# Dense work beside attention in steps of 512 tokens in place of 256, with weight conversions spread, the product with v in one run, and tau loaded first

## The chip, the cores and the metric

One core of one Trainium2 chip runs the kernel; the other cores are idle. The metric is the device time of one execution in microseconds. TensorE (PE, with its weight loads PEld), VectorE (DVE), ScalarE (ACT), GpSimd (POOL) and SyncE (SP) each run their own queue of instructions in order and wait for one another by semaphores. All DMAs of this kernel are issued from SP.

## The reference

Sparse attention followed by two dense blocks, all in float32. Four batches, eight heads, 576 tokens, head size 64:

```python
scores = q @ k.T / 8
thresh = max(scores) - tau
scores = where(scores >= thresh, scores, -1e9)
attn = exp(scores - max(scores)); attn = attn / (sum(attn) + 1e-9)
x = (attn @ v), heads joined: 2304 tokens x 512
h = x @ w_in1                      # 512 -> 2048
g = h where h >= 1, 0 where h <= -1, else (h + 1)**2 / 4
x = g @ w_out1                     # 2048 -> 512
h = x @ w_in2
out = (h * clip(h + 3, 0, 6) / 6) @ w_out2
```

The weights arrive as 64-bit floats, of which the kernel reads the two 32-bit halves.

## The kernel before, in words

**Attention** goes by jobs: 16 of them, one for each batch and pair of heads (`jobs`), with five row blocks each (128, 128, 128, 128 and 64 query rows), so 80 steps, and three more steps to drain. In a step `t` the generator `attention` (L407) issues, with a `yield` after each part: the scores of a block (`em_scores`: matmuls at L284, a pass out of PSUM with the row minimum of the negated scores at L296, exp at L300, a small add at L303, mask and row sum at L306); the turned tail of the block two steps back (`em_tail`); up to three chunks of the product with v (`pv_run(3)`, L420); at certain blocks the normalisation of the job before (`em_norm`, which writes x to DRAM and marks the job done) or the turning of the next q or k; then the transposes of the block one step back, for two heads (`em_pt`), with two more product chunks between them (`pv_run(2)`, L438). A job's blocks are gathered in two groups, and each group's product with v has five chunks (`pv_chunk`, L361), for 32 groups in all.

**Dense work beside attention** is `dense1` (L605). It does part of the first dense block, the first 10 of its 16 blocks of hidden units (`NF1`), for the 512 main tokens of batches 0 to 2, in six groups of 256 tokens (`GRP`). A float32 product is made from three passes (`hi*hi`, `hi*lo`, `lo*hi`) in the type fp32r. `em_h` makes a hidden block: 4 x 3 matmuls of 128x128 weights by 256 tokens (L485) into one PSUM bank, Q2 while attention runs (`H_TAGS`), then two ScalarE steps and one VectorE step of the activation (L494 to L496) and its split in `gh` and `gl` (L502, L503). `em_part` does the second matmul (L542): two of the four output blocks side by side in bank Q3, summed over ten hidden blocks, then copied out (L551, L553) and written to `x2p`. `split_x` loads x (L460) and splits it (L468, L469). `steps` lists which output pieces follow which hidden block; what is left after the last hidden block is issued by `behind` in the next phase. The sum over the other six hidden blocks is added there.

**The order** around this is set by hand. The main loop (L711) runs attention from yield to yield. Until batch 0 is ready it converts weights: `weights.half()` once a step and twice in every third step. Each conversion of one weight block has two halves: `split_a` (ScalarE L111 and L114, GpSimd L115, VectorE L122) and `split_b` (VectorE L128, GpSimd L130, L133 and L137; beside dense work ScalarE L135 in place of L133). Loads run up to three blocks ahead (`RAW`). From then on each yield earns 0.57 of credit, which pays for pieces of dense work at 0.33 each (three matmuls of 256 columns); weights not yet converted are converted when `ahead1` asks for them. Tile's planner orders each engine's queue with a timeline of its own from this program, so issue order is a priority and not the exact order; `after` pins one instruction behind another on its engine. `pin_mlp` pins the first matmul of a dense piece behind an attention matmul.

**Afterwards** the same first dense block follows for batch 3 and the 256 tail tokens, then the remaining six hidden blocks for batches 0 to 2, then the second dense block, all in steps of 512 tokens (256 for the tail group).

Of the kernel before, what the change touches and what calls it, by code (L numbers as in the profile page):

```python
# [18 lines left out]
def kernel(  # L19
# [12 lines left out]
    nc = tc.nc  # L32
# [23 lines left out]
    mt = mt_es.enter_context(tc.tile_pool(name="mt", bufs=2, side="right"))  # L56
# [8 lines left out]
    xd, x2p, x2d = ([dram.tile([128, KD, n], F32, name=f"{nm}{w}") for w, n in enumerate(WIDE)]  # L65
                    for nm in ("xd", "x2p", "x2d"))

    def narrow(t, g):
        return t[g // 2][:, :, (g % 2) * GRP:(g % 2 + 1) * GRP]
# [34 lines left out]
    def split_a(kind, m, f):  # L104
# [12 lines left out]
        else:  # L117
# [4 lines left out]
        V.tensor_scalar(out=c, in0=c, scalar1=3, scalar2=0x3FFFFFFF,  # L122
                        op0=ALU.logical_shift_left, op1=ALU.bitwise_and)
        wc[kind, m, f] = (hi, lo, c, t, r)

    def split_b(kind, m, f):
        hi, lo, c, t, r = wc.pop((kind, m, f))
        V.scalar_tensor_tensor(out=c, in0=t[:, :, 1], scalar=0xC0000000, in1=c,  # L128
                               op0=ALU.bitwise_and, op1=ALU.bitwise_or)
# [141 lines left out]
    def em_scores(j, i):  # L271
# [135 lines left out]
    def attention():  # L407
# [3 lines left out]
        for t in range(n + 3):  # L411
# [8 lines left out]
            pv_run(3)  # L420
# [17 lines left out]
            pv_run(2)  # L438
# [12 lines left out]
    def split_x(key, kks=range(KD)):  # L451
        m, g, ph = key
        r = xs.setdefault(key, [])
        for kk in kks:
            if kk < len(r):
                continue
            if ph == 1:
                if kk % 2 == 0:
                    t = mt.tile([128, 2, GRP], F32, tag="io", name="xst", bufs=2)
                    nc.sync.dma_start(out=t, in_=narrow(xd, g)[:, kk:kk + 2, :])  # L460
                pool, n, bufs, src = mt, GRP, 1, t[:, kk % 2]
            else:
                pool, n, bufs = wide["x"], WIDE[g], 2
                src = pool.tile([128, n], F32, tag="xst", name="xst", bufs=3)
                nc.sync.dma_start(out=src, in_=(x2d if m == 1 else xd)[g][:, kk, :])
# [10 lines left out]
    def em_h(key, m, f):  # L476
        cnt["h"] += 1
        n = GRP if key[2] == 1 else WIDE[key[1]]
# [3 lines left out]
        for kk in range(KD):  # L482
# [6 lines left out]
            if kk < KD - 1:  # L489
                yield 0.33  # L490
        hp_, hb = (mt, HOLD) if key[2] == 1 else (wide["g"], MLAG + 1)
        r = hp_.tile([128, n], F32, tag="r", name="r", bufs=2)
# [38 lines left out]
    def em_part(key, half, f):  # L531

        gh, gl = gs[key, f] if half == 0 else gs.pop((key, f))
        wh, wl = wsp["o", 0, f]
        if f == 0:
            acc[key] = bank("Q3")
        a = acc[key]
        for i in range(2):
            c = slice((2 * half + i) * 128, (2 * half + i + 1) * 128)
            o = a[:, i * GRP:(i + 1) * GRP]  # L540
            for x, (l, r) in enumerate(((wh[:, c], gh), (wh[:, c], gl), (wl[:, c], gh))):
                mm = T.matmul(o, l, r, start=(f == 0 and x == 0 and i == 0),  # L542
                              stop=(f == NF1 - 1 and x == 2 and i == 1), skip_group_check=True)
                if x == 0:
                    pin_mlp(mm)
            if i == 0:
                yield 0.33
        if f == NF1 - 1:
            ob = mt.tile([128, 512], F32, tag="io", name="ob", bufs=2)
            if half:  # L550
                S.activation(out=ob, in_=acc.pop(key), func=ACTF.Copy)  # L551
            else:
                V.tensor_copy(out=ob, in_=acc.pop(key))  # L553
            nc.sync.dma_start(
# [267 lines left out]
```

## Time and profile before

| | us |
|---|---|
| median of 3 runs | 1200.21 |
| lowest, highest | 1199.99, 1202.96 |
| the profiled execution | 1200.08 |
| its span, first to last instruction | 1198.3 |

The page gives, for each engine, the time in which it was busy, as a share of the span. Groups of instructions are named by line, engine, operation and tiles (written <- read), with shapes in partitions x elements; then the count, the busy time, the mean duration, and how long the engine was idle just before them and what ended that. A matmul's duration in the profile includes its way through the array, where the next one already runs behind it, so the distance between the starts of two matmuls is what one costs in a run. The chain of waits is the work that ended last, followed back from the last instruction in a stretch.

### The profile page before, as it was taken

Reading aid. Unit: us, or ns where it says so; the run is one execution under the profiler, and the core shown is the slowest. Engines: PE = TensorE matmul, PEld = TensorE weight load, DVE = VectorE, ACT = ScalarE, POOL = GpSimd, SP = SyncE. Lnnn points to the kernel's source line nnn. Section 1 sums busy time; section 2 is a strip of 40 time slices with the busy share of each in tenths; the row PEclk is TensorE's granted clock in tenths of the full one; section 3 lists DMA queues with packets and bytes.
Section 4 is the critical chain, followed back from the end, with each engine's and each line's share of the span. In section 5 each row is a group of like instructions: output and inputs, shape, how many; then the busy total and the mean of one; then the engine's idle time right before and its main releaser. Section 6 shows DMA issues by size and latency. Waiting matters only on the chain.

```text
span 1198.3 us, 17942 instructions
## 1 busy us (share of the span) xinstructions
PE 1138.7 (95%) x6656; PEld 906.7 (76%) x6656; DVE 579.6 (48%) x1196; ACT 627.5 (52%) x1217; POOL 418.8 (35%) x397
## 2 busy tenths in 40 slices
PE   4877799998999999999999999999999999999998
PEld 3444477876777787777888988888888888888886
DVE  3899865456555565553652575555740121121111
ACT  4667766565665665664665676654542222233222
POOL 1767531110111111112673666656742213222221
PEclk9999889999999999999999999999999999999999
DMA  4444421212111222003431244453210010010000
GB/s 114 117 133 135 128 81 30 51 50 59 54 35 31 59 59 68 21 20 107 149 103 47 81 136 150 152 168 98 88 43 15 1 58 9 1 44 2 18 1 35
DMA packets 106791, 82.43 MB, mean 69 GB/s; under 512 B 66512, under 2 KB 90576, under 8 KB 106704
## 3 DMA queue, kind: packets, MB, share of 16 engines
q1 hardware_dynamic: 106704, 81.29, 23.0%
q8 instruction: 52, 0.85, 0.3%
q14 instruction: 35, 0.29, 0.1%
HBM read 63.96 MB, written 17.30 MB: 68 GB/s over the span
## 4 chain that ended last, share of the span: by engine, by line
PE 83%; DVE 6%; ACT 4%; DMA 3%; SPq 2%; issue 2%; POOL 0%; ACTq 0%; DVEq 0%
PE Q L485 33%; PE P L527 26%; PE Q L542 7%; PE Q L361 6%; PE P L284 5%; PE Q L244 5%; DVE p L306 2%; DVE p L296 2%; DMA w_raw<-in_moe_w_in_dram 1%; PE P L244 1%; ACT e L300 1%; DMA w_raw<-in_moe_w_out_dram 1%; DVE w_c L122 1%; ACT r L494 1%; DVE w_c L128 1%
## 5 line engine op out<-in xcount | busy, mean ns | idle before, releaser
L503 POOL TENSOR_TENSOR gl<-r,gh 128x512 fp32r<-128x512 f32 (+1 forms) x190 | 205.9, 1084 | 641.7 <-ACT gh L502 624.1
L485 PE MATMUL Q<-xh,wih 128*128 128x512 f32 (+1 forms) x760 | 264.5, 349 | 0.7 <-ACT xh L468 0.5
L485 PE MATMUL Q<-xl,wih 128*128 128x512 f32 (+1 forms) x760 | 257.8, 339 | 0.2 <-DVE xl L469 0.2
L485 PE MATMUL Q<-xh,wil 128*128 128x512 f32 (+1 forms) x760 | 257.6, 339 | 0.0
L499 DVE SCALAR_TENSOR_TENSOR r<-r,Q 128x512 f32<-128x512 f32 (+1 forms) x80 | 50.7, 633 | 248.9 <-ACT r L498 248.8
L485 PEld LDWEIGHTS Q<-xh,wih 128*128 128x128 f32 x760 | 144.7, 191 | 29.9 <-issue 10.6
L502 ACT ACTIVATE gh<-r 128x512 fp32r<-128x512 f32 (+1 forms) x190 | 99.9, 526 | 121.5 <-PE P L527 53.3
L485 PEld LDWEIGHTS Q<-xl,wih 128*128 128x128 f32 x760 | 144.8, 191 | 16.5 <-DVE xl L469 0.7
L485 PEld LDWEIGHTS Q<-xh,wil 128*128 128x128 f32 x760 | 144.6, 190 | 15.6 <-issue 0.5
L296 DVE TENSOR_SCALAR_CACHE_REDUCE p<-P 128x576 f32<-128x576 f32 x144 | 104.1, 753 | 80.0 <-PE Q L244 71.5
L306 DVE SCALAR_TENSOR_TENSOR p<-p,th,e 128x576 f32<-128x576 f32 x144 | 130.9, 923 | 24.0 <-ACT e L300 17.4
L244 PE MATMUL Q<-ident,p 128*128 128x128 f32 (+1 forms) x656 | 113.8, 287 | 21.1 <-DVE p L306 10.1
L300 ACT ACTIVATE e<-p,nm 128x576 f32<-128x576 f32 x144 | 109.8, 773 | 32.7 <-DVE p L296 31.6
L498 ACT ACTIVATE r<-Q,three 128x512 f32<-128x512 f32 (+1 forms) x80 | 51.4, 643 | 143.4 <-PE Q L485 140.3
L244 PEld LDWEIGHTS Q<-ident,p 128*128 128x128 f32 (+1 forms) x656 | 74.6, 143 | 63.0 <-DVE p L306 11.7
L284 PE MATMUL P<-kt,qt 64*128 64x288 f32 (+1 forms) x640 | 109.1, 450 | 13.7 <-DVE p L296 7.5
L496 DVE SCALAR_TENSOR_TENSOR r<-r,Q 128x256 f32<-128x256 f32 (+1 forms) x110 | 55.0, 500 | 131.9 <-ACT r L495 129.5
L527 PE MATMUL P<-woh,gh 128*128 128x512 f32 x288 | 111.9, 390 | 0.6 <-DVE ob L580 0.6
L527 PE MATMUL P<-wol,gh 128*128 128x512 f32 x288 | 112.2, 390 | 0.0
L527 PE MATMUL P<-woh,gl 128*128 128x512 f32 x288 | 110.9, 390 | 0.0
L130 POOL TENSOR_TENSOR w_c<-w_c,w_raw 128x512 int32<-128x512 int32 x64 | 87.4, 1366 | 39.3 <-DVE w_c L128 28.1
L327 ACT ACTIVATE Gf<-Q 128x512 f32<-128x512 f32 x128 | 75.0, 591 | 48.6 <-PE Q L244 48.5
(81 smaller groups left out, 1865.2 us busy)
## 6 DMA issues: line engine op xcount, KB each, us to landing
w_raw<-in_moe_w_in_dram SPq DMA_DIRECT2D x32, 512.0 KB, 3.8
w_raw<-in_moe_w_out_dram SPq DMA_DIRECT2D x32, 512.0 KB, 3.6
xst<-xd SPq DMA_DIRECT2D x28, 256.0 KB, 3.2
kn<-in_k_dram SPq DMA_DIRECT2D x32, 128.0 KB, 2.6
qn<-in_q_dram SPq DMA_DIRECT2D x32, 128.0 KB, 2.6
vn<-in_v_dram SPq DMA_DIRECT2D x32, 128.0 KB, 2.6
xd<-xu SPq DMA_DIRECT2D x16, 256.0 KB, 2.5
x2d<-ob SPq DMA_DIRECT2D x16, 256.0 KB, 3.4
```

What stands on the lines that cost most here:

```text
L130: x = G.tensor_tensor(out=c.bitcast(I32), in0=c.bitcast(I32), in1=r, op=ALU.add)
L244: x = T.transpose(out, in_, ident)
L284: mm = T.matmul(o, qt[j][r, c], kt[j][r, k0:k0 + HS], start=True, stop=True, skip_group_check=True)
L296: V.tensor_scalar(out=p[:, x], in0=s[:, :, 0:HS], scalar1=-1.0, scalar2=3e38, op0=ALU.mult, op1=ALU.min, accum_out=nm[:, x:x + 1])
L300: S.activation(out=e, in_=p[:, x], func=ACTF.Exp, bias=nm[:, x:x + 1], scale=-1.0)
L306: V.scalar_tensor_tensor(out=p[:, x], in0=p[:, x], scalar=th[:, x:x + 1], in1=e, op0=ALU.is_le, op1=ALU.mult, accum_out=zt[j][:, z:z + 1])
L327: S.activation(out=f[:, h, :, d0:d0 + 128], in_=tm.rearrange("p (c n) -> p c n", c=4), func=ACTF.Copy)
L485: mm = T.matmul(h, l[:, kk * 128:(kk + 1) * 128], r, start=(x == 0), stop=(x == 3 * KD - 1))
L502: x = S.activation(out=gh, in_=r, func=ACTF.Copy)
L503: y = G.tensor_tensor(out=gl, in0=r, in1=f32(gh), op=ALU.subtract)
L527: T.matmul(a, l, r, start=(first and x == 0), stop=(last and x == 2))
L542: mm = T.matmul(o, l, r, start=(f == 0 and x == 0 and i == 0), stop=(f == NF1 - 1 and x == 2 and i == 1), skip_group_check=True)
```

## The change

The groups of dense work beside attention are 512 tokens, one for each of batches 0 to 2. `em_h` makes 4 x 3 matmuls of 512 columns. `em_part` makes one output block of 512 tokens for one hidden block; a bank holds one output block only, so its sum is split in two runs of five hidden blocks (`SUB`): the first is written to a new DRAM tensor `x2q`, and the second reads it back, adds it, and writes `x2p`. Output pieces alternate with the quarters of a hidden block, 18 behind (`OFF`), and while a batch isn't ready, waiting pieces are issued. A piece of three 512-column matmuls costs 0.62 of credit. Conversions go one half a step, before dense work begins and beside it, pinned behind the step's exp (ScalarE) and masking (VectorE). All five chunks of a product with v are issued at one place. Tau's load is the first DMA. Pools are cut to fit.

```diff
-    GRP = 256
-    NG = (NB - 1) * MAIN // GRP
+    NG = NB - 1
...
+    SUB = 5
...
-        V.tensor_scalar(out=c, in0=c, scalar1=3, scalar2=0x3FFFFFFF,
-                        op0=ALU.logical_shift_left, op1=ALU.bitwise_and)
+        x = V.tensor_scalar(out=c, in0=c, scalar1=3, scalar2=0x3FFFFFFF,
+                            op0=ALU.logical_shift_left, op1=ALU.bitwise_and)
+        if mode["att"]:
+            after(x, pins["V"])
...
-            S.activation(out=e, in_=p[:, x], func=ACTF.Exp, bias=nm[:, x:x + 1], scale=-1.0)
+            pins["S"] = S.activation(out=e, in_=p[:, x], func=ACTF.Exp, bias=nm[:, x:x + 1], scale=-1.0)
...
-            V.scalar_tensor_tensor(out=p[:, x], in0=p[:, x], scalar=th[:, x:x + 1], in1=e,
-                                   op0=ALU.is_le, op1=ALU.mult, accum_out=zt[j][:, z:z + 1])
+            pins["V"] = V.scalar_tensor_tensor(
+                out=p[:, x], in0=p[:, x], scalar=th[:, x:x + 1], in1=e,
+                op0=ALU.is_le, op1=ALU.mult, accum_out=zt[j][:, z:z + 1])
...
-            pv_run(3)
             yield
...
-            pv_run(2)
+            pv_run(5)
...
+            n = WIDE[g]
             if ph == 1:
-                if kk % 2 == 0:
-                    t = mt.tile([128, 2, GRP], F32, tag="io", name="xst", bufs=2)
-                    nc.sync.dma_start(out=t, in_=narrow(xd, g)[:, kk:kk + 2, :])
-                pool, n, bufs, src = mt, GRP, 1, t[:, kk % 2]
+                pool, bufs = xt, 1
+                src = mt.tile([128, n], F32, tag="io", name="xst", bufs=2)
...
+    def em_part(g, sub, i, f):
+
+        key = (0, g, 1)
+        lasti = i == KD - 1
+        gh, gl = gs.pop((key, f)) if lasti else gs[key, f]
         wh, wl = wsp["o", 0, f]
+        if f % SUB == 0:
+            cnt["a"] += 1
+            acc[key] = bank("Q3" if mode["att"] or cnt["a"] % 2 else "Q1")
+            if sub:
+                pbs[key] = mt.tile([128, MAIN], F32, tag="io", name="pb", bufs=2)
+                nc.sync.dma_start(out=pbs[key], in_=x2q[g][:, i, :])
         a = acc[key]
+        c = slice(i * 128, (i + 1) * 128)
+        for x, (l, r) in enumerate(((wh[:, c], gh), (wh[:, c], gl), (wl[:, c], gh))):
+            mm = T.matmul(a, l, r, start=(f % SUB == 0 and x == 0), stop=(f % SUB == SUB - 1 and x == 2))
+            if x == 0:
+                pin_mlp(mm)
+        if f % SUB == SUB - 1:
+            del acc[key]
+            if sub:
+                ob = pbs.pop(key)
+                V.tensor_tensor(out=ob, in0=a, in1=ob, op=ALU.add)
+            else:
+                ob = mt.tile([128, MAIN], F32, tag="io", name="ob", bufs=2)
+                if i % 2:
+                    S.activation(out=ob, in_=a, func=ACTF.Copy)
+                else:
+                    V.tensor_copy(out=ob, in_=a)
+            nc.sync.dma_start(out=(x2p if sub else x2q)[g][:, i, :], in_=ob)
...
+    outs = [(g, sub, i, sub * SUB + f) for g in range(NG) for sub in range(NF1 // SUB)
+            for i in range(KD) for f in range(SUB)]
+    n_out = len(outs)
+    OFF = 4 * SUB - 2
+    HOLD = max(u // 4 for u in [OFF + o - 4 * (g * NF1 + f) for o, (g, _, i, f) in enumerate(outs) if i == KD - 1])
+    PIECE = 0.62
...
                 while not ready(g):
-                    yield None
+                    if outs[0][0] < g:
+                        weights.upto(2 * NF1)
+                        em_part(*outs.pop(0))
+                        yield PIECE
+                    else:
+                        yield None
                 split_x(key)
             ahead(n, f)
+            h = em_h(key, 0, f)
+            for kk in range(KD):
+                next(h, None)
+                if f == NF1 - 1 and kk == KD - 1:
+                    xs.pop(key)
+                    if g + 1 < NG and ready(g + 1):
+                        split_x((0, g + 1, 1))
...
+                yield PIECE
+                if n_out - len(outs) < 4 * n + kk + 1 - OFF:
+                    em_part(*outs.pop(0))
+                    yield PIECE
...
+    nc.sync.dma_start(out=taus[:, 2:3], in_=tau.to_broadcast([128, 1]))
     load_k(0)
     load_q(0)
-    nc.sync.dma_start(out=taus[:, 2:3], in_=tau.to_broadcast([128, 1]))
...
                 weights.half()
-                if mode["t"] % 3 == 0:
-                    weights.half()
             if not ready(0):
                 continue
             mode["mlp"] = True
+        elif mode["step"] and weights.done < 2 * NF1:
+            mode["step"] = False
+            weights.half()
```

## Rows read from the trace of the kernel before

**Rows 1.** The page, part 1: busy us, share of the span, instructions

```profile
PE 1138.7 (95%) x6656; PEld 906.7 (76%) x6656; DVE 579.6 (48%) x1196; ACT 627.5 (52%) x1217; POOL 418.8 (35%) x397
```

**Rows 2.** Busy by stage (us): PE, PEld, DVE, ACT, POOL; granted clock; DMA

```profile
42.00:140.00 98.00, 75.52 (x466) 44.35 (x466) 87.68 (x190) 67.03 (x135) 65.93 (x65) 0.92 0.44 124
...
160.00:553.00 393.00, 384.18 (x2842) 295.55 (x2838) 211.05 (x583) 238.30 (x518) 55.16 (x79) 0.99 0.16 43
```

**Rows 3.** L303 (once a step of attention) by stage: us, DVE busy (count)

```profile
42.00:140.00 98.00, 5.58 (x17) 0.92 0.44 124
...
160.00:534.00 374.00, 11.87 (x53) 0.99 0.17 45
```

**Rows 4.** Groups, 42 to 140 us: count | busy, mean | idle before

```profile
L306 DVE SCALAR_TENSOR_TENSOR p<-p,th,e 128x576 f32<-128x576 f32 x31 | 36.6, 1197 | 6.2 <-ACT e L300 5.3
...
L122 DVE TENSOR_SCALAR w_c<-w_c 128x512 uint32<-128x512 uint32 x15 | 11.4, 763 | 1.2 <-POOL w_c L115 1.2
...
L128 DVE SCALAR_TENSOR_TENSOR w_c<-w_raw,w_c 128x512 uint32<-128x512 uint32 x15 | 10.6, 706 | 0.1
L111 ACT ACTIVATE w_raw<-w_raw 128x512 int32<-128x512 uint32 x15 | 10.2, 682 | 9.7 <-DMA w_raw<-in_moe_w_in_dram 5.9 <-DMA w_raw<-in_moe_w_out_dram 3.9
```

**Rows 5.** Groups, 200 to 500 us, same columns

```profile
L306 DVE SCALAR_TENSOR_TENSOR p<-p,th,e 128x576 f32<-128x576 f32 x80 | 65.2, 829 | 11.4 <-ACT e L300 7.0
```

**Rows 6.** Chain of waits, 42 to 140 us, shares by line

```profile
by line: DVE p L306 22.5%; DVE p L296 11.9%; issue 10.3%; DMA w_raw<-in_moe_w_out_dram 7.8%; DVE w_c L122 6.3%; ACT e L300 5.9%; DVE w_c L128 5.2%; DMA w_raw<-in_moe_w_in_dram 4.7%; POOL w_c L130 3.2%; DVE th L303 2.7%; ACT w_c L114 2.3%; D
```

**Rows 7.** Groups of the whole span, shapes apart, columns as in rows 4

```profile
L542 PE MATMUL Q<-gh,woh 128*128 128x256 f32 x240 | 75.2, 313 | 0.3
...
L496 DVE SCALAR_TENSOR_TENSOR r<-r,Q 128x512 f32<-128x512 f32 x34 | 23.3, 684 | 60.6 <-ACT r L495 59.7 <-DMA w_raw<-in_moe_w_out_dram 0.8
L494 ACT ACTIVATE r<-Q,half 128x512 f32<-128x512 f32 x34 | 23.0, 680 | 9.0 <-PE Q L485 5.2 <-POOL gl L503 3.4
L495 ACT ACTIVATE r<-r 128x512 f32<-128x512 f32 x34 | 21.2, 628 | 0.6
...
L553 DVE COPY ob<-Q 128x512 f32<-128x512 f32 x6 | 4.1, 690 | 6.6 <-PE Q L542 6.5
```

**Rows 8.** TensorE's timeline (start us, us), 21 matmuls, first and last

```profile
656.80 0.28 PE L485 MATMUL Q<-xh,wih 128*128 128x256 f32 x1
...
659.19 0.28 PE L485 MATMUL Q<-xh,wil 128*128 128x256 f32 x1
```

**Rows 9.** TensorE's timeline, 24 matmuls, first and last, same columns

```profile
722.82 0.39 PE L527 MATMUL P<-gh,woh 128*128 128x512 f32 x1
...
728.03 0.39 PE L527 MATMUL P<-gh,wol 128*128 128x512 f32 x1
```

**Rows 10.** L485, then L542, 160 to 554 us: PE and PEld busy

```profile
160.00:554.00 394.00, 105.43 (x684) 88.61 (x685) 0.99 0.16 43
...
160.00:554.00 394.00, 102.06 (x642) 84.13 (x642) 0.99 0.16 43
```

**Rows 11.** Timeline of all engines, 402 to 408 us [idle before <-releaser]

```profile
402.33 0.36 PE L485 MATMUL Q<-xh,wil 128*128 128x256 f32 x1
...
403.63 0.19 PEld L542 LDWEIGHTS Q<-gh,woh 128*128 128x128 f32 x1 [0.38 <-issue]
...
404.12 0.42 DVE L496 SCALAR_TENSOR_TENSOR r<-r,Q 128x256 f32<-128x256 f32 x1 [2.61 <-ACT r L495]
...
407.16 0.28 PE L485 MATMUL Q<-xh,wih 128*128 128x256 f32 x1
```

**Rows 12.** DMA issues, loads of x: count, KB each, us to landing

```profile
xst<-xd SPq DMA_DIRECT2D x28, 256.0 KB, 3.2
```

**Rows 13.** Timeline of all engines at the start [idle before <-releaser]

```profile
7.38 0.59 SPq L678 DMA_DIRECT2D taus<-in_tau_dram  x1
...
8.56 1.33 PE L244 MATMUL P<-ident,qn 128*128 128x128 f32 x5 [0.85 <-DMA qn<-in_q_dram]
...
10.67 0.74 ACT L256 ACTIVATE qt<-P,taus 128x576 f32<-128x576 f32 x1 [2.22 <-DVE taus L687]
```

More of the change, by code (lines that the diff above doesn't have):

```diff
@@ L529, in em_out @@
             fin(key[1], a, i)
-    def em_part(key, half, f):
-        gh, gl = gs[key, f] if half == 0 else gs.pop((key, f))
+    def em_part(g, sub, i, f):
+        key = (0, g, 1)
+        lasti = i == KD - 1
+        gh, gl = gs.pop((key, f)) if lasti else gs[key, f]
         wh, wl = wsp["o", 0, f]
-        if f == 0:
-            acc[key] = bank("Q3")
-        a = acc[key]
[L538 to L551, printed above, removed]
-            else:
-                V.tensor_copy(out=ob, in_=acc.pop(key))
-            nc.sync.dma_start(
-                out=narrow(x2p, key[1])[:, 2 * half:2 * half + 2, :],
-                in_=ob.rearrange("p (k n) -> p k n", k=2))
@@ L591 @@
     n_h = NG * NF1
-    outs = [(g, half, f) for g in range(NG) for half in range(2) for f in range(NF1)]
-    OFF = NF1 + 2 * MLAG - 3
-    steps, o = [], 0
-    while o < len(outs):
-        n = len(steps)
-        steps.append([])
-        while o < len(outs) and (o < 2 * (n + 1) - OFF or n >= n_h) and outs[o][0] * NF1 + outs[o][2] + MLAG <= n:
-            steps[-1].append(outs[o])
-            o += 1
-            if n >= n_h and len(steps[-1]) == 2:
-                break
-    HOLD = 1 + max(n - g * NF1 - f for n, l in enumerate(steps) for g, half, f in l if half)
+    outs = [(g, sub, i, sub * SUB + f) for g in range(NG) for sub in range(NF1 // SUB)
[4 more added lines that the diff above has]
+    PIECE = 0.62
     def dense1(ready, ahead):
-        for n, l in enumerate(steps[:n_h]):
+        for n in range(n_h):
             g, f = divmod(n, NF1)
@@ L611, in dense1 @@
                 while not ready(g):
[L612 removed]
+                    if outs[0][0] < g:
[4 more added lines that the diff above has]
+                        yield None
                 split_x(key)
             ahead(n, f)
[L615 to L625 removed]
+            h = em_h(key, 0, f)
[5 more added lines that the diff above has]
+                        split_x((0, g + 1, 1))
+                if n == n_h - 3 and kk == KD - 1 and not mode["att"]:
+                    split_x((0, NB - 1, 2))
+                yield PIECE
+                if n_out - len(outs) < 4 * n + kk + 1 - OFF:
+                    em_part(*outs.pop(0))
+                    yield PIECE
     def behind():
[L629 to L632 removed]
+        while outs:
+            em_part(*outs.pop(0))
+            if len(outs) % 4 == 0:
                 yield
@@ L672, in ready @@
     def ready(g):
-        return all(g // 2 * HP + hp in done_jobs for hp in range(HP))
+        return all(g * HP + hp in done_jobs for hp in range(HP))
+    nc.sync.dma_start(out=taus[:, 2:3], in_=tau.to_broadcast([128, 1]))
     load_k(0)
@@ L696 @@
     first_use = {("i", f): f for f in fs1}
-    for n, l in enumerate(steps):
-        for x in l:
-            first_use.setdefault(("o", x[2]), n)
+    for o, x in enumerate(outs):
+        first_use.setdefault(("o", x[3]), (o + OFF) // 4)
     by_use = sorted(first_use, key=lambda x: (first_use[x], x))
@@ L741 @@
         pass
+    xt_es.close()
+    wide["g"] = g_es.enter_context(tc.tile_pool(name="g1", bufs=1))
     seq2 = [(g, f) for g in (NB - 1, NB) for f in range(KF)]
```

46 lines of the change are left out of this document (16 added, 30 removed).

## The prediction

> **What bounds the kernel now.** I read the page first, then busy time by stage, then the instruction groups and the chain of waits inside each stage. TensorE is busy 95% of the span [rows 1], but that mean hides two regimes. From 42 to 140 us attention runs alone: TensorE is busy 75.5 of 98 us, and VectorE 87.7 of 98 [rows 2]. From 160 to 553 us dense work fills TensorE beside attention: it is busy 384 of 393 us, VectorE 211 and ScalarE 238 [rows 2]. After that the kernel is plain dense work, which the change touches only at its beginning. So an edit pays in the first stage if it takes time off VectorE or off the chain through it, and in the second if it takes time off TensorE.
>
> In the first stage a step of attention (one row block of one head pair) takes 98/17 = 5.76 us, in the second 374/53 = 7.06 us [rows 3]. Weight conversions are what crowds the first: 15 of them lie in those 17 steps, each with 0.76 and 0.71 us on VectorE, and ScalarE stands 9.7 us in front of them until a weight has landed, with attention's exponentials queued behind [rows 4]. GpSimd is busy 65.9 of the 98 us, and meanwhile the masking instruction (L306) takes 1197 ns [rows 4]; later, with GpSimd busy 55 of 393 us [rows 2], it takes 829 ns [rows 5]. Conversions and their loads make up 7.8 + 6.3 + 5.2 + 4.7 + 3.2 + 2.3 = 29.5% of this stretch's chain [rows 6].
>
> **The change part by part.** The sum is made against the profiled execution, 1200.08 us (span 1198.3 and 1.8 around it); the median of the runs shown is 0.13 us above it.
>
> *Fewer conversions first.* Before, a step issues one half conversion and every third step another, so 14 are issued by step 23, and the trace has nearly all 20 done by 160 us. After, it is one half a step, pinned behind the step's exponential and masking: 10 or 11 by step 23. The rate per step falls from 15/17 = 0.88 to 0.5. On VectorE that takes off 0.38 x 1.47 = 0.56 us a step. The stretching of L306, 31 x 0.37 us over 17 steps = 0.67 us a step, should shrink with GpSimd's load by 43%, or 0.29 us. VectorE's 87.7/17 = 5.16 us becomes 4.31, and at the same busy share a step takes 4.84: 0.92 us less, 15.7 us in 17 steps. By the chain instead, 43% of 29.5% of 98 us is 12.4. I take **-14**. Ends: -5, if what stays (loads, exponentials, the waits between engines) sets the pace, and -20, if the 9.7 us of standing in front of loads goes as well, since a slower rate leaves three prefetched weights ahead.
>
> *Where they go.* Ten conversions move into steps 23 to 36, which TensorE bounds. There they find ScalarE at 61% and VectorE at 54% [rows 2]. ScalarE's part is about 0.68 for the first operation [rows 4] and two more like it, 2 us a weight: some 0.7 weights a step make 1.4 us more on its 238/55.7 = 4.3 of 7.06 us. That cover holds, though both queues run in order, so a transposed block can be copied out late: **+2**; ends 0 and 10.
>
> *512 columns.* Dense work beside attention has 60 x 12 matmuls of 256 columns in its first half (from the code) and 3 x 240 in its second [rows 7]; 720 of 512 replace 1440. In a run of 256-column matmuls starts are (659.19 - 656.80)/20 = 0.1195 us apart [rows 8], in one of 512 (728.03 - 722.82)/23 = 0.2265 [rows 9]. A pair saves 0.0125 us: 720 pairs, **-9**, all on TensorE. Ends -6 (pairs mixed with attention save less) and -10. The Trainium skill, "TensorE: Matmul & The Clock Gate", section "Back-to-back issue gap", gives a stream N/2.4 ns and a fixed 2.5 ns a matmul; by that a pair would save 2.5 ns and this term would be -1.8, the sum 1193. The rows speak against it: 256 columns more cost 226.5 - 119.5 = 107 ns, so of the 119.5 about 12.5 are a fixed part.
>
> *How much dense work fits beside attention.* By the code a step has 4.4 yields of 0.57 credit. It paid for 7.6 pieces of three 256-column matmuls at 0.33, and now pays for 4.05 of three 512-column ones at 0.62: by rows 8 and 9, 7.6 x 0.359 = 2.72 us before and 4.05 x 0.680 = 2.75 after, no difference. But 222 of 240 pieces are then spent by step 78 (18 outputs lag behind for the dense phase), so the last five steps and the drain run without filler. Attention alone takes TensorE 393 us less 1326 x 0.1195 [rows 10], over 393/7.06 = 55.7 steps, or 4.2 us a step, near its VectorE pace above, and the 18 late pieces (12.2 us) fill the drain: **+2**; ends 0 and 6.
>
> *Product with v in one run.* Each of 32 products was issued as three and two chunks, now as five: one switch between products and dense matmuls less. Behind one such run the next weight load stood 0.38 us [rows 11], but the array was still finishing meanwhile; I count 0.1 us for the 24 in the stage that TensorE bounds: **-2**; ends 0 and -9.
>
> *The bank of the first half.* While attention runs, one PSUM bank (Q2) takes every hidden block. Before, the last matmul of a block started at 402.33, the bank was read out at 404.54, and the next block began at 407.16 [rows 11]. So the chain that reads it took 2.2 us, three instructions and the waits between them. With 512 columns L496 grows from 0.42 us to 0.68 [rows 7] and L494 and L495 about as much, so the chain takes 2.9 to 3.0. In the order written, what lies between is no longer all outputs together but one output piece (0.68) and about 2.2 yields of attention (4.2/4.4 us of TensorE's time each): 2.8. That is no cover to spare, for 30 blocks, although later output pieces can be planned ahead: **+4**; ends 0 and 30.
>
> *More evictions, reloads, transitions.* Splitting the second half's sum in two makes 24 evictions of 0.69 us [rows 7] in place of 12, 12 reloads and 24 writes in place of 12. The engines that do them have room, and SP issues only some 24 DMAs more in 400 us. But bank Q3 is single as well, and its next sum starts after its eviction: **+1**; ends 0 and 8. At the second and third batch the output pieces are drained while waiting, and new x must land (3.2 us [rows 12]) before dense work resumes; the third batch did not have that: **+2**.
>
> *Tau first.* The scaled q waits 2.22 us for tau; but q's transposes end only at 8.56 + 1.33 = 9.89 against 10.67, and tau's issue of 0.59 now stands ahead of all of q and k on SP [rows 13], so q comes at 10.48: **-0.2**.
>
> The sum: -14 - 9 - 2 - 0.2 + 2 + 2 + 4 + 1 + 2 = -14.2, or **1186 us**.
>
> **Rivals.** *The bank turnaround becomes the bound (slower).* If each of 30 hidden blocks holds TensorE for 1.0 us at Q2, because an instruction like L111 on ScalarE (0.68 [rows 4]) and one masking on VectorE (0.83 [rows 5]) stand ahead in queues that run in order, and two thirds of that reach TensorE, the term is 30, not 4: 1212 us. It decides against the change from about 0.6 us a block. For it: cover and chain come out equal. Against: the gap of 4.8 us in rows 11 shows the planner putting other work between. Chance 0.13.
> *The first stage hardly moves.* Its pace is latency, as the 10.3% "issue" and 12.5% loads in rows 6 might say, and the conversions disturb the second stage: -5 in place of -14, +6 in place of +2, so 1199. Against: VectorE is 89% busy there. Values between this and the forecast are likelier than the point itself, about 1192 to 1200. Chance 0.19.
> *The first stage falls further,* to 4.3 us a step, VectorE's bare load, with loads all early (0.5 x 17 = 9 us more) and the bank free (4 more): 1173. Chance 0.12.
> *A pair saves next to nothing.* If columns alone set the distance of starts, 1440 short matmuls take no longer than 720 long ones, the term falls from -9 to between 0 and -2, and the time is 1193 to 1195. The page cited above would have it so. Against: rows 8 and 9. Chance 0.02.
> *The forecast itself,* 1179 to 1192: 0.54.
>
> **How the numbers follow.** A measurement of this kernel can tell about 0.3%, 3.6 us, from no change: faster is below 1196.6, slower above 1203.8. Faster: 0.54, 0.12, 0.02 and 0.11 of the second rival's 0.19, together 0.79; the same, 0.08; slower, 0.13, the first rival. The range of 8 in 10 reaches from the strong first stage to the weak one: 1171 to 1199. Outside lie the first rival and the ends of the others.
>
> **What would show it.** Right: the step in the first stage (spacing of L303) falls from 5.76 to about 4.8 us, L306 there nearer 1.0 us, some ten conversions after dense work begins, no matmul of 256 columns before the tail group's, and TensorE as full as before in the second stage. Wrong: a step of 5.5 us or more there; idle time on PE before hidden-block matmuls ended by L496; TensorE idle for more than some microseconds around the end of attention; or, in the second stage, steps longer than 7 us at the same share of dense work.

## The result, and the profile after

| | before | after |
|---|---|---|
| median of 4 runs, us | 1200.92 | 1216.96 |
| lowest, highest | 1199.99, 1202.96 | 1212.97, 1220.59 |
| the profiled execution | 1200.08 | 1212.97 |
| its span | 1198.3 | 1211.1 |

After stands to before as 1.013, interval 1.0093 to 1.0168: 1.3% slower, where 1186 and faster were forecast. The profiled execution of after is the fastest of its four, 4 us below their median, so differences between its trace and others come out smaller than those between medians; e2, e3, e6 and e10 below were profiled in one of their slower executions (2 to 5 us above their medians). By the intervals, a difference of a later run to after is known to some 5 us, one between two of the later runs to 3 or 4. The function names below are those of the listing; lines are after's: L247 (transposes), L287 (scores), L303 (exp), L306 (the small add), L309 (masking), L299 (row minimum), L365 (product with v), L470 and L471 (split of x), L487 (hidden block), L498 (the last of the activation's three steps; L496 in before), L548 (output piece), L331 (copy of a transposed block out of its bank).

The page's part 1 for after, then busy time by stage, columns as in [rows 2], and that view for L306, once a step of attention, as in [rows 3]:

```profile
PE 1128.9 (93%) x5936; PEld 859.6 (71%) x5936; DVE 572.0 (47%) x1166; ACT 610.8 (50%) x1119; POOL 401.2 (33%) x363
```

Busy time by stage in after:

```profile
42.00:140.00 98.00, 73.57 (x481) 46.98 (x483) 77.72 (x187) 62.06 (x121) 39.82 (x42) 0.93 0.36 99
...
160.00:571.00 411.00, 379.71 (x2173) 251.69 (x2171) 226.24 (x568) 232.90 (x446) 76.53 (x76) 0.99 0.24 69
```

L306 alone in after:

```profile
42.00:140.00 98.00, 4.87 (x18) 0.93 0.36 99
160.00:557.00 397.00, 14.43 (x54) 1.00 0.24 69
```

TensorE has 10 us less to do over the span [rows 1], as 720 longer matmuls for 1440 should give. But in the first stage VectorE lost 10 of its 87.7 us and GpSimd 26 of its 65.9 [rows 2], and 98 us still hold only 18 steps, not 20. And in the second stage TensorE is idle for 31 of 411 us, where it was idle for 9 of 393.

The working over the whole kernel is best read at three points of the trace: the starts of L306 in steps 25 and 79 (counted from 0), and the end of the span. The later experiments stand in the same table; "pace" is the mean distance of those starts from step 5 to 20, before dense work begins.

| us | pace | to step 25 | step 25 to 79 | to the end | last two |
|---|---|---|---|---|---|
| before | 5.76 | 157.7 | 376.5 | 664.1 | 1040.6 |
| after | 5.58 | 154.7 | 402.2 | 654.2 | 1056.4 |
| e1, split of x pinned | 5.26 | 150.6 | 395.3 | 654.6 | 1049.9 |
| e2, credit 0.53 | 5.66 | 156.4 | 385.5 | 660.6 | 1046.1 |
| e3, product in two places | 5.42 | 155.2 | 399.0 | 654.9 | 1053.9 |
| e5, all three | 4.84 | 145.8 | 378.8 | 658.2 | 1037.0 |
| e6, e5 with the product in one place | 5.41 | 151.0 | 380.4 | 660.6 | 1041.0 |
| e9, e5 without drained pieces | 4.84 | 145.4 | 374.9 | 665.7 | 1040.6 |
| e4, before with new conversions | 5.18 | 143.5 | 380.3 | 665.1 | 1045.4 |
| e8, e4 with split of x pinned | 4.84 | 145.1 | 382.5 | 664.4 | 1046.9 |
| e7, before, product in one place | 5.89 | 161.4 | 373.7 | 664.9 | 1038.6 |
| e10, e4, product in one place | 5.45 | 158.1 | 381.9 | 665.3 | 1047.2 |

The forecast put 14 us of gain left of step 25 and nothing, in sum, right of it. It came to 3 us of gain and 15.8 us of loss. So two things are to be found: what kept the first stage at 5.58 us a step, and what the second stage lost.

**The first stage.** Groups of instructions, 42 to 140 us, columns as in [rows 4]:

```profile
L309 DVE SCALAR_TENSOR_TENSOR p<-p,th,e 128x576 f32<-128x576 f32 x33 | 34.4, 1056 | 3.9 <-ACT e L303 1.9 <-DVE th L306 0.5
...
L129 DVE SCALAR_TENSOR_TENSOR w_c<-w_raw,w_c 128x512 uint32<-128x512 uint32 x9 | 6.2, 685 | 0.0
...
L121 DVE TENSOR_SCALAR w_c<-w_c 128x512 uint32<-128x512 uint32 x9 | 4.6, 509 | 0.0
...
L471 DVE TENSOR_TENSOR xl<-xst,xh 128x512 fp32r<-128x512 f32 x3 | 2.1, 693 | 7.4 <-ACT xh L470 7.4
L470 ACT ACTIVATE xh<-xst 128x512 fp32r<-128x512 f32 x3 | 1.9, 629 | 9.9 <-DMA xst<-xd 9.9
```

What the forecast wanted to go went: nine conversions in place of 15, the masking at 1056 ns in place of 1197, ScalarE's 9.7 us in front of weights no longer listed. In their place stands a new row: ScalarE waits 9.9 us, in three pieces, for x to land, and VectorE 7.4 us for ScalarE. The chain of waits of the same stretch:

```profile
by line: DVE p L309 12.9%; DVE p L299 10.6%; DMA xst<-xd 10.5%; PE P L287 10.4%; DMA xd<-xu 8.3%; PE Q L247 6.9%; issue 4.8%; PE P L247 3.9%; ACT e L303 3.4%; ACT Gf L331 3.3%; PE Q L365 2.9%; DMA kn<-in_k_dram 2.4%; DVE xl L471 2.1%; ACT x
...
110.69 2.43 DMA xd<-xu
113.19 3.51 DMA xst<-xd
```

The write of x to DRAM and its reading back are 18.8% of the chain, 18.4 of 98 us, in three pairs (from 53.75, 82.53 and 110.69 us). [rows 6] has neither. The timeline shows how a load for work that begins at 133.8 us can stop attention at 114:

```profile
110.69 0.33 SPq L403 DMA_DIRECT2D xd<-xu  x1
...
113.19 0.32 SPq L467 DMA_DIRECT2D xst<-xd  x1
...
116.72 0.63 ACT L470 ACTIVATE xh<-xst 128x512 fp32r<-128x512 f32 x1 [3.15 <-DMA xst<-xd]
...
117.26 0.76 ACT L303 ACTIVATE e<-p,nm 128x576 f32<-128x576 f32 x1
117.38 0.69 DVE L471 TENSOR_TENSOR xl<-xst,xh 128x512 fp32r<-128x512 f32 x1 [2.30 <-ACT xh L470]
...
118.81 1.92 PE L287 MATMUL P<-kt,qt 64*64 64x288 f32 x8 [2.90 <-DVE p L299]
```

A job's x is written at 110.69, read back at 113.19, and lands at 116.7. The planner placed the split of this 512-token block in ScalarE's queue right there. The queue runs in order: attention's exp (L303) gets its turn at 117.26, VectorE stands in front of L471, and TensorE waits 2.90 us for a scores bank. With groups of 256 tokens two jobs of heads shared a load; with 512, each of batch 0's four jobs has a load of its own, and its wait stands in the queue as soon as the job is done. The VectorE halves of the splits run at 91.6, 93.0, 149.7 and 150.1 us in before, two behind every second job, and at 60.6, 89.6, 117.4 and 146.3 in after.

**The second stage.** Busy time in five stretches; the steps 40 to 44 and 60 to 64 are the first and third, the drain the last. In after:

```profile
270.00:307.00 37.00, 32.78 (x194) 21.82 (x194) 21.83 (x58) 20.75 (x40) 2.01 (x3) 1.00 0.29 83
...
418.00:455.00 37.00, 32.82 (x193) 21.52 (x193) 21.15 (x57) 20.26 (x40) 2.01 (x3) 1.00 0.28 86
...
530.00:577.00 47.00, 40.05 (x222) 25.60 (x221) 20.86 (x55) 21.74 (x44) 6.13 (x6) 0.96 0.20 65
```

The same view of before, steps 40 to 44, 60 to 64, and 75 to the drain:

```profile
270.00:306.00 36.00, 32.47 (x219) 22.81 (x219) 19.81 (x56) 19.81 (x43) 3.60 (x5) 0.95 0.19 50
...
409.00:442.00 33.00, 32.95 (x252) 25.68 (x251) 21.05 (x57) 22.24 (x49) 4.75 (x7) 1.00 0.20 54
...
510.00:554.00 44.00, 43.59 (x335) 34.73 (x334) 18.14 (x51) 24.32 (x55) 5.61 (x9) 1.00 0.06 18
```

Before filled TensorE in steps 60 to 64 and in the drain to within 0.5 us; after leaves 4.2 and 7.0 us open. There dense work is missing: in after, hidden blocks pause from 249.5 to 284.3 and from 399.2 to 427.8 us, and only drained output pieces run. (In steps 40 to 44 before has 3.5 us open as well.) After each pause they come in lumps (TensorE's timeline; all 12 matmuls of a hidden block stand between two runs of attention):

```profile
299.24 1.23 PE L287 MATMUL P<-kt,qt 64*128 64x288 f32 x6
300.40 0.50 PE L487 MATMUL Q<-xh,wih 128*128 128x512 f32 x1
...
303.07 0.40 PE L487 MATMUL Q<-xh,wil 128*128 128x512 f32 x1
303.31 0.60 PE L247 MATMUL Q<-ident,p 128*128 128x128 f32 x4
```

The eleven starts are (303.07 - 300.40)/11 = 0.243 us apart, with nothing between. In the middle of the stage, 0.232 is usual. The steps behind the pauses are the longest against before: 45 to 49 take 8.66 us (before 7.07), 65 to 69 take 8.21 (6.78). But they also hold more dense work, as much as 10.8 pieces of 256 columns a step where before has 8.4 and 7.8, so most of that is work moved and not time lost.

### The profile page after: what moved, and what is told of

It reads as the page before. It is cut to its first block, busy times and chain, and to the rows that moved or that the text cites. A ratio compares the mean times of both kernels' runs of the same rounds, so it can differ in the third digit from the quotient of the medians.

```text
span 1211.1 us, 16285 instructions
## 1 busy us (share of the span) xinstructions
PE 1128.9 (93%) x5936; PEld 859.6 (71%) x5936; DVE 572.0 (47%) x1166; ACT 610.8 (50%) x1119; POOL 401.2 (33%) x363
## 4 chain that ended last, share of the span: by engine, by line
PE 75%; DVE 8%; ACT 6%; DMA 4%; POOL 3%; issue 3%; SPq 1%; DVEq 0%; POOLq 0%; ACTq 0%
PE Q L487 29%; PE P L529 24%; PE Q L548 6%; PE P L287 6%; PE Q L365 5%; PE Q L247 4%; DVE p L299 3%; DVE p L309 2%; DMA xst<-xd 1%; PE P L247 1%; DMA xd<-xu 1%; ACT e L303 1%; ACT r L496 1%; DVE w_c L129 1%; POOL w_c L133 1%
## 5 line engine op out<-in xcount | busy, mean ns | idle before, releaser
L505 POOL TENSOR_TENSOR gl<-r,gh 128x512 fp32r<-128x512 f32 (+1 forms) x160 | 197.9, 1237 | 574.6 <-ACT gh L504 570.7
L487 PE MATMUL Q<-xh,wih 128*128 128x512 f32 (+1 forms) x640 | 241.3, 379 | 6.5 <-DVE r L498 3.7
L487 PE MATMUL Q<-xl,wih 128*128 128x512 f32 (+1 forms) x640 | 236.6, 370 | 0.1
L487 PE MATMUL Q<-xh,wil 128*128 128x512 f32 (+1 forms) x640 | 236.3, 369 | 0.0
L299 DVE TENSOR_SCALAR_CACHE_REDUCE p<-P 128x576 f32<-128x576 f32 x144 | 104.3, 754 | 113.3 <-PE Q L247 80.5
L504 ACT ACTIVATE gh<-r 128x512 fp32r<-128x512 f32 (+1 forms) x160 | 93.9, 587 | 111.6 <-PE P L529 52.0
L487 PEld LDWEIGHTS Q<-xh,wih 128*128 128x128 f32 x640 | 121.1, 189 | 35.9 <-issue 5.9
L247 PE MATMUL Q<-ident,p 128*128 128x128 f32 (+1 forms) x656 | 115.0, 290 | 31.0 <-ACT Gf L331 15.5
L287 PE MATMUL P<-kt,qt 64*128 64x288 f32 (+1 forms) x640 | 112.5, 451 | 26.0 <-DVE p L299 20.6
L309 DVE SCALAR_TENSOR_TENSOR p<-p,th,e 128x576 f32<-128x576 f32 x144 | 126.1, 892 | 22.3 <-ACT e L303 14.5
L247 PEld LDWEIGHTS Q<-ident,p 128*128 128x128 f32 (+1 forms) x656 | 77.0, 144 | 82.8 <-ACT Gf L331 24.1
L487 PEld LDWEIGHTS Q<-xh,wil 128*128 128x128 f32 x640 | 120.8, 189 | 20.2
L487 PEld LDWEIGHTS Q<-xl,wih 128*128 128x128 f32 x640 | 120.9, 189 | 19.4 <-DVE xl L471 0.6
L303 ACT ACTIVATE e<-p,nm 128x576 f32<-128x576 f32 x144 | 109.4, 771 | 44.3 <-DVE p L299 43.6
L287 PEld LDWEIGHTS P<-kt,qt 64*128 64x128 f32 (+1 forms) x640 | 57.2, 185 | 65.0 <-DVE p L299 25.4
L331 ACT ACTIVATE Gf<-Q 128x512 f32<-128x512 f32 x128 | 75.0, 590 | 49.4 <-PE Q L247 49.0
```

What stands on the lines that cost most here:

```text
L247: x = T.transpose(out, in_, ident)
L287: mm = T.matmul(o, qt[j][r, c], kt[j][r, k0:k0 + HS], start=True, stop=True, skip_group_check=True)
L299: V.tensor_scalar(out=p[:, x], in0=s[:, :, 0:HS], scalar1=-1.0, scalar2=3e38, op0=ALU.mult, op1=ALU.min, accum_out=nm[:, x:x + 1])
L303: pins["S"] = S.activation(out=e, in_=p[:, x], func=ACTF.Exp, bias=nm[:, x:x + 1], scale=-1.0)
L309: pins["V"] = V.scalar_tensor_tensor(out=p[:, x], in0=p[:, x], scalar=th[:, x:x + 1], in1=e, op0=ALU.is_le, op1=ALU.mult, accum_out=zt[j][ ...
L331: S.activation(out=f[:, h, :, d0:d0 + 128], in_=tm.rearrange("p (c n) -> p c n", c=4), func=ACTF.Copy)
```

## The experiments

Three theories of the loss were set against the forecast's rival of bank Q2: the split of x stands in front of attention; the credit spends dense work before the next batch is there; the product with v, in one place, holds TensorE.

**The split of x, pinned** (e1, an edit of after). It may no longer go ahead of the step's exp and masking.

```diff
-            S.activation(out=hi, in_=src, func=ACTF.Copy)
-            V.tensor_tensor(out=lo, in0=src, in1=f32(hi), op=ALU.subtract)
+            x = S.activation(out=hi, in_=src, func=ACTF.Copy)
+            y = V.tensor_tensor(out=lo, in0=src, in1=f32(hi), op=ALU.subtract)
+            if mode["att"]:
+                after(x, pins["S"])
+                after(y, pins["V"])
```

> The changed kernel with one edit: while attention runs, the split of a loaded block of x (ScalarE copy, VectorE subtraction) is pinned behind the last exp and the last masking issued, so the planner can't hoist it into the first stage. Theory A (the first stage kept its pace because each of batch 0's four x blocks is now loaded and split as soon as its job is done, and ScalarE stands in front of each load with the exponentials queued behind): the chain of 42 to 140 us loses its 18.8% of x transfers, a step there falls from about 5.6 to 4.8 us, and the time falls by 10 to 18 us, to 1199 to 1207. Theory B (latency of attention's own chain sets that pace): the step stays at 5.5 us or more and the time within 4 us of the changed kernel's.

Measured: 1204.12 us, 1.0022 of before (1.0007 to 1.0037): 12.8 less than after. ScalarE's waits for x, in after up to 150 us and from 150 to 560, then in e1 (us in total, times, longest):

```profile
ACT xh L470 <- DMA xst<-xd: 9.9, 3, 3.5
...
ACT xh L470 <- DMA xst<-xd: 9.3, 7, 2.7
```

In e1:

```profile
ACT xh L470 <- DMA xst<-xd: 0.8, 1, 0.8
...
ACT xh L470 <- DMA xst<-xd: 2.2, 3, 1.2
```

So the theory of the hoisted split is shown: without these waits 12.8 us are gone. The table puts 4.1 us of it ahead of step 25 and 6.5 after; the latter are almost all in steps 40 to 44 and 60 to 64 (7.27 to 6.63 and 7.38 to 6.75 us a step), where batches 1 and 2 get their x. The first stage did not reach the 4.8 that was forecast, and its chain says what stands there next:

```profile
by line: DVE p L309 17.2%; DVE p L299 13.1%; PE Q L365 11.7%; PE P L287 8.6%; issue 7.1%; PE Q L247 5.5%; ACT Gf L331 4.8%; ACT e L303 3.8%; DMA xst<-xd 3.5%; POOL wil L140 3.0%; DVE th L306 2.7%; POOL w_c L133 2.7%; DVE w_c L129 2.5%; DVE 
...
82.14 4.00 PE Q L365 x20
```

The loads fell from 10.5 to 3.5%, and the product with v (L365), one run of 20 matmuls, rose from 2.9 to 11.7%. Of the 4.00 us in the line above, a part ran at a lower granted clock (0.57 on average); the same 20 matmuls took 2.31 us at 54.63, at 1.00.

**Less credit** (e2, an edit of after): `share = 0.57` becomes `share = 0.53`.

> The changed kernel with the credit of a yield at 0.53 in place of 0.57, so that the dense pieces last to the end of attention and don't run ahead of batch 2. Theory C (the second stage lost its time where dense work is missing: from step 60 while batch 2 isn't ready and after step 78, since attention alone can't fill TensorE): attention's own time on TensorE falls from 4.79 to about 3.8 us a step in steps 60 to 64 and from 5.6 to 4.3 in the last ones, and the time falls by 8 to 15 us. Theory D (512-column pieces and the single bank of the hidden blocks hold TensorE everywhere): those steps get shorter and others longer, and the time stays within 4 us.

Measured: 1199.86, 0.9988 (0.9974 to 1.0001): 17.1 less than after, and no different from before. Stage times in the table: 16.7 us less between steps 25 and 79, 6.4 more behind, because some dense work now falls there. Steps 60 to 64 take 6.26 us (after 7.38), and 75 to 79 with the drain 43 us (47). Steps 75 to the drain, in e2's own time:

```profile
519.00:562.00 43.00, 41.36 (x240) 28.08 (x241) 21.56 (x55) 22.71 (x46) 6.29 (x6) 1.00 0.16 55
```

1.6 us are open in place of 7.0. So the credit cost time, by more than the 8 to 15 us expected. How much is less sure: the two profiled executions are only 8.5 us apart.

**The product in two places again** (e3, an edit of after).

```diff
+            pv_run(3)
             yield
...
-            pv_run(5)
+            pv_run(2)
```

> The changed kernel with the product with v issued as three and two chunks again. If five at one place took away work that covered the hand-over of bank Q0 between the turned tail and the transposes, the time falls by 3 to 8 us; if one run saves switches, as the prediction had it, the time rises by 1 to 4 us.

Measured: 1208.36, 1.0061 (1.0039 to 1.0083): 8.6 less than after. One place costs time, where a gain of 2 was forecast. Here too the profiled executions (2.0 us apart in the table) show less than the medians.

**The conversions alone, in before** (e4): of the whole change only one half a step, and its pins.

```diff
                 weights.half()
-                if mode["t"] % 3 == 0:
-                    weights.half()
...
+        elif mode["step"] and weights.done < 2 * NF1:
+            mode["step"] = False
+            weights.half()
```

> The kernel before with the conversions' part of the change alone: one half a step, also beside dense work, pinned behind the step's exp and masking. By the prediction's term the first stage gains 14 us and the second loses 2: 1186 to 1192. By Theory B (attention's own latency sets the first stage's pace) the time stays at 1196 to 1206. Here x is loaded for two jobs at a time, so only one load of it can fall into the first stage; a gain of 10 us or more here and none in the changed kernel would speak for Theory A.

Measured: 1190.47, 0.9912 (0.9894 to 0.9931): 11.4 less than before. By the table 14.2 us are won ahead of step 25 and 4.8 given back behind. The step's pace is 5.18. (Two loads of x fall into its first stage, from 79.34 and 132.12 us, not the one expected.) So the forecast's first term, with the one for where the conversions go (-14 + 2), was right in sum where nothing else was changed, though the pace is not yet the 4.84 that was worked out for it.

**All three edits** (e5: after with e1, e2 and e3) and **the same with the product in one place** (e6: after with e1 and e2).

> The changed kernel with all three edits at once: x's split pinned, 0.53 of credit, the product with v as three and two chunks. If the three losses are separate, their gains add (13, 17 and 9 us off the changed kernel's 1217): 1176 to 1184. If two of them are one (for instance the stalls around batch 2 and the late product), the time is 1185 to 1198.

> The same without the third edit, so with five chunks of the product with v at one place. Against the run with three and two chunks: 6 to 10 us longer if the one place costs by itself, within 3 us if it cost only together with the missing dense work.

Measured: e5 1184.75, 0.9869 of before (0.9851 to 0.9888), the fastest kernel of the study; e6 1191.44, 0.9924 (0.9896 to 0.9952), 6.7 more. Singly the edits gave 12.8 + 17.1 + 8.6 = 38.5, together 32.2, between the two ranges expected. Two of them work on the same steps 40 to 44 and 60 to 64, which would explain the difference; but each sum has after's uncertainty in it several times over, so it isn't shown. In the first stage it looks the other way round: the pin alone takes 0.32 us off the pace, the product alone 0.16, both with the credit 0.74, as if each stood behind the other. The chain of the first stage in e6:

```profile
by line: DVE p L309 14.1%; PE Q L365 12.6%; DVE p L299 11.6%; PE P L287 10.7%; PE Q L247 8.5%; issue 6.1%; ACT Gf L331 5.0%; ACT e L303 4.4%; POOL w_c L133 4.0%; DMA xst<-xd 3.5%; POOL wil L140 3.0%; DVE w_c L129 2.5%; DVE th L306 2.2%; PE 
...
99.10 4.19 PE Q L365 x20
...
108.60 2.31 PE Q L365 x20
```

The same in e5:

```profile
by line: DVE p L309 18.5%; DVE p L299 15.1%; PE Q L365 13.1%; PE P L287 7.4%; issue 5.8%; DMA kn<-in_k_dram 5.1%; ACT e L303 4.9%; PE P L247 3.9%; PE Q L247 3.5%; DVE w_c L129 3.1%; DVE th L306 2.7%; DVE w_c L121 2.5%; PE Q L491 2.3%; SPq L
...
102.36 2.00 PE Q L365 x12
```

The product's own share hardly differs. What differs is that in e6 the transposes and scores behind the 20 matmuls (L247, L287) hold 19.2% of the chain, in e5, behind 12, 10.9%. TensorE's waits up to 560 us say the same (us in total, times, longest). In e6:

```profile
PE Q L247 <- ACT Gf L331: 14.7, 12, 5.2
```

In e5:

```profile
PE Q L247 <- ACT Gf L331: 3.9, 8, 0.9
```

A transpose waits until ScalarE has copied its bank out (L331). In two places the product's chunks fill two of these gaps; in one they fill one, and hold transposes and scores behind the whole run. Which of the two counts more, the gap left open or the length of the run, was not tried apart.

A third thing differs, and it wasn't tried apart either: the granted clock. Around the two runs of 20 matmuls shown above, e6 has (the granted clock is the third number from the right):

```profile
99.10:103.30 4.20, 4.20 (x21) 1.84 (x22) 4.06 (x9) 2.43 (x4) 2.88 (x3) 0.68 0.01 2
108.60:110.90 2.30, 2.30 (x22) 1.34 (x22) 1.61 (x4) 0.62 (x2) 0.57 (x1) 1.00 0.37 129
```

So part of the 4.19 us comes from the lower clock, not from the length of the run. From 42 to 140 us the granted clock is 0.93 in e6 and 0.98 in e5. Up to step 25, TensorE stood at the lower level (1.2 in place of 2.4 GHz) for 20.5 us in e6 and 10.2 in e5. If all that runs there takes twice as long, this is worth some 5 us, an estimate and an upper bound, of the 5.2 that e6 loses up to that step. So the one place is shown to cost time, but whether by what waits behind it or by the clock stays open.

**The product in one place, in before** (e7) **and in before with the new conversions** (e10); the edit is e3's, reversed.

> The kernel before with the five chunks at one place and nothing else. If what they covered was the hand-over of bank Q0, in the first stage above all, where no dense work lies between: 3 to 9 us longer than before. By the prediction's term: 2 us shorter.

> The kernel before with the conversions' part and the five chunks at one place. The one place cost 6.7 us in the version with x pinned and 0.53, but 1.7 in the kernel before. If it costs only once conversions no longer set the first stage's pace: 4 to 8 us above the run with the conversions' part alone (1190), with most of it before dense work begins. If it costs only with pieces of 512: within 2 us of 1190.

Measured: e7 1202.28, 1.0014 (1.0000 to 1.0029), some 1.7 us more than before, less than the 0.3% that a measurement can tell; e10 1203.67, 1.0026 (1.0010 to 1.0042), 13.2 more than e4. So the cost comes with the fewer conversions. A reading that fits: while they set the pace (5.76), a held TensorE is late for nothing; at 5.18 it is late. The table puts nearly all of e10's loss ahead of step 25. The chain of the first stage in e4:

```profile
by line: DVE p L310 16.1%; DVE p L300 13.5%; ACT e L304 9.9%; PE Q L365 7.5%; issue 6.4%; PE P L288 6.1%; DMA xst<-xd 6.0%; DMA xd<-xu 6.0%; ACT Gf L331 4.1%; PE Q L248 2.9%; DVE w_c L130 2.5%; DMA kn<-in_k_dram 2.3%; ACT w_raw L111 1.8%; D
```

In e10:

```profile
by line: PE Q L365 16.2%; PE P L288 15.0%; DVE p L310 10.7%; PE Q L248 10.3%; DVE p L300 9.4%; issue 6.2%; ACT e L304 4.6%; ACT Gf L331 3.9%; PE P L248 3.6%; DMA xd<-xu 3.0%; DMA xst<-xd 3.0%; ACT qt L260 1.5%; ACT w_c L114 1.4%; POOL w_c L
```

(Lines are one higher here: L248 transposes, L288 scores, L300 row minimum, L304 exp, L310 masking.) VectorE and ScalarE lead in e4, TensorE's product and scores in e10. The clock differs here as well: up to step 25, 34.1 us at the lower level in e10 and 13.7 in e4, by the same estimate at most some 10 of the 14.6 us lost there.

**The split of x, pinned, in before with the new conversions** (e8).

> The kernel before with the conversions' part and x's split pinned, so all that the better versions share except steps of 512. The two loads of x left in its first stage cost some 12% of that stretch's chain, so 3 to 8 us below the run with the conversions' part alone (1190). Against the version of 512 with the same edits it shows what 512 columns are worth by themselves: by the prediction's term that one is 9 us shorter; if coarser pieces and one bank cost what the fixed part of a matmul saves, they are within 4 us.

Measured: 1194.04, 0.9941 (0.9920 to 0.9962), 3.6 more than e4; the gain expected was missed. The pace improves, 5.18 to 4.84, and steps 20 to 24, where dense work begins, take 6.08 us in place of 4.95, so that nothing is left at step 25. The gain was given back at the transition; why these steps are longer was not tried. Against e8, e5 is 9.3 us shorter (against e4 5.7). It differs by tau and by all that came with steps of 512: the columns, the split sum, the order of the output pieces, the credit and the smaller pools. So 9.3 is what these are worth together, known to some 3 us; the columns alone weren't tried.

**No output pieces while a batch isn't ready** (e9, an edit of e5).

```diff
                 while not ready(g):
-                    if outs[0][0] < g:
-                        weights.upto(2 * NF1)
-                        em_part(*outs.pop(0))
-                        yield PIECE
-                    else:
-                        yield None
+                    yield None
```

> The version with all three edits, and the 18 waiting output pieces no longer issued while batches 1 and 2 aren't ready, so that they are left to go between the next batch's first hidden blocks. Theory E (right after such a drain dense work has hidden blocks alone; each must wait for the single bank Q2, and nothing fills TensorE meanwhile): the five steps after it fall from 8.3 us to about 7.2, TensorE's attention time there from 4.1 to 3.6 a step; the time falls by 2 to 6 us. Theory F (the drained pieces are worth more where they are, since steps 38 to 43 and 59 to 63 have no other dense work): those steps lose what the later ones gain or more, and the time rises by 0 to 8 us.

Measured: 1187.80, 0.9898 (0.9876 to 0.9919), 3.0 more than e5. Kept back, the pieces lie between the hidden blocks later on: steps 45 to 49 fall from 8.32 to 7.67 us, 65 to 69 from 8.20 to 7.17. But stretches without them, and the phase behind (665.7 in place of 658.2 us), lose more. So draining while waiting is no loss, and probably a gain: the 3.0 us are hardly clear of noise.

## Why the prediction was wrong

The number, 1186, is not far from e5's 1184.75, but that is another kernel; for this one three steps of the working failed.

- **Fewer conversions first, -14: right by itself, and hidden here.** e4 shows it (14.2 us ahead of step 25), and e5, together with its other edits, comes to 11.9; e5's and e8's pace is the 4.84 that the prediction worked out, e4's 5.18. The granted clock, which the working left out, may have a part in that: between steps 5 and 20 TensorE stands at the lower level for 13.7 us in before, 10.2 in e4 and not at all in e5 and e8. In after only 3 us arrived. The failing step is an item that the sum didn't have: the loads of x, one for each job with 512 tokens, were looked at for the third batch only ("+2"), as something dense work waits for, not as something placed in ScalarE's queue ahead of attention. [rows 4] showed the pattern, ScalarE standing 9.7 us in front of weights; the same question had to be put to every load whose user shares attention's queue. Measured by e1: 12.8 us in all. Ahead of step 25 the pin gives back 4.1 of the 11 us missing there; with the lower credit it is 3.7 (e6), and 5.2 more come with the product in two places (e5).
- **How much dense work fits beside attention, +2: wrong.** The prediction compared TensorE's time for a step, 2.72 and 2.75 us, and concluded "no difference". But 4.05 pieces of 512 columns are 8.1 pieces of 256, against 7.6: 6.6% more work a step. Work is limited by the batches' coming ready, so it runs out before the next batch. Keeping 7.6 half-pieces needs 0.57 x 0.62/0.66 = 0.535, which is e2's 0.53. It measured 17.1 us alone. The +2 looked for the loss at the end, where after leaves 7.0 us open, and not at the batches, where it leaves 4.2 us open twice.
- **Product with v in one run, -2: wrong sign.** The step counted switches, in the stage that TensorE bounds. e7 does show 2.0 us less there and behind (1040.6 to 1038.6), no more than executions of one kernel differ by, but the first stage, not considered, loses 3.7 in e7 and 14.6 in e10, and in e6 there is nothing won behind (1041.0 against 1037.0). Measured: +6.7 to +13.2 once the conversions are fewer, part of it perhaps by the clock.
- **512 columns, -9: right in sign, and near in size.** Starts beside attention are usually 0.120 us apart at 256 columns and 0.232 at 512. A pair so saves 0.008 us and 720 pairs some 6, the term's near end. With what comes between the runs, the distances from each dense matmul to the next start add up to 191.8 us up to 553 (before) and 183.7 up to 571 (after), 8 less. The fourth rival has a pair save next to nothing; 0.008 us speaks against it. The Trainium skill, "TensorE: Matmul & The Clock Gate", section "Back-to-back issue gap", gives N/2.4 + 2.5 ns for an isolated matmul, and says that in a stream of weight loads and matmuls both set the spacing. The prediction took the formula for a stream; by it a pair saves 2.5 ns, by estimate 1.8 us in all, and this trace, with 8 ns, doesn't agree.
- **The bank of the first half, +4, and the slower rival:** the sign was the rival's, the mechanism wasn't; that its 1212 us is near the measured 1217 is luck. Its 30 us should stand in TensorE's waits for L498. Up to 560 us, in after, these are (total, times, longest):

```profile
PE Q L487 <- DVE r L498: 3.7, 6, 1.0
```

  and those of its weight loads from 150 to 600 us:

```profile
PEld Q L487 <- DVE r L498: 5.9, 9, 1.1
```

  So at most about 6 us, the weight load and its matmul waiting for the same thing: near the 4.
- **Where the conversions go, +2:** the 4.8 us in e4 fit between its ends. **Evictions and reloads, transitions, tau** weren't tried alone; nor were the smaller pools. The first small add (L306, in before L303) starts at 15.16 to 15.26 us in the seven kernels with tau first and at 15.26 to 15.29 in the five without, a gain of some 0.1 for the -0.2.

Of what the prediction said would show it wrong, two held: a step of 5.5 us in the first stage, and TensorE idle around the end of attention. The steps of the second stage were longer too (402.2/54 = 7.4 us), but not at the same share of dense work.

## What to carry to other kernels

When a block gets bigger, ask of each of its loads when its data is there, whose in-order queue its first user stands in, and what else is behind it; a planner that sees the load as early puts the wait there. A filler paid by credit must be priced in work, not in time, and its supply set against when the next input comes ready. Edits that each remove the second-longest wait look useless or harmful singly: price them where the wait ahead of them is gone, as e7 and e10 do, and undo each part of a slow change before throwing it away, for here three small edits turn 1217 us into 1185.

## What the runs showed of the hardware

- The masking (L309), whose operands are all in SBUF, has 1197 ns with GpSimd busy 67% of the stretch [rows 2, 4] and 1056 with 41%; in e5, with 43%, 979, so GpSimd's share isn't the whole of it. The row minimum L299, which reads PSUM, has 749 ns in the same stretch of before, 751 in after and in e5.
- A load's wait isn't a loss by itself: e5 has ScalarE stand 16.5 us in front of x between 150 and 560 us, more than after's 9.3, where ScalarE has room (in e5 it is busy 228 of 385 us from 160 us on), and is 32 us faster.
- The granted clock falls after the loads' stops. TensorE in after by stretches of 10 us (busy, granted clock), from 50 us:

```profile
50.00:60.00 10.00, 7.14 (x55) 1.00 0.43 114
60.00:70.00 10.00, 7.63 (x36) 0.66 0.27 72
70.00:80.00 10.00, 8.29 (x59) 1.00 0.37 98
80.00:90.00 10.00, 5.57 (x42) 1.00 0.42 124
90.00:100.00 10.00, 7.17 (x41) 0.83 0.37 93
```

  After the stops at 53.75 and 82.53 us it is 0.66 and 0.83 in the following ten (0.87 after the third, from 120 us), that is, part of them at 1.2 in place of 2.4 GHz, and 36 and 41 matmuls run where 55 and 59 did. In 42 to 140 us after has 0.93, e1 and e5 0.98: some of what the pin gives back may come by the clock, how much wasn't separated. The stops aren't its only occasion: before has 0.92 there without them, e6 0.93 with x's split pinned.
